# Bucket writes one by one in VectorE's written order, and conditional slots' output writes behind all blocks

## The chip, the cores and the metric

The kernel runs on one core of one Trainium2 chip. The metric is device time in microseconds, from the first to the last instruction of one launch; lower is better. The profile is one further execution of the same program with the hardware profiler on.

## The reference

Two stages in float32. The first is attention with a sliding window over 8 batches, 8 heads, 576 positions and 64 channels. Half of the heads see the last 32 positions, the other half every fourth of the last 128. The second is a mixture of experts without dropped tokens over the 4608 tokens that come out (512 channels each, 8 experts, 1024 hidden channels):

```python
scores = scale * q @ k.T                       # per batch and head
scores = np.where(mask, scores, -1e9)          # plain or dilated window
x = softmax(scores) @ v                        # -> (4608, 512)
logits = x @ w_gate
expert_idx = np.argmax(logits, axis=1)
gate_w = softmax(logits)[arange(N), expert_idx]
for e in range(8):                             # tokens of expert e
    y[tokens_e] = np.maximum(x[tokens_e] @ w1[e], 0) @ w2[e]
out = gate_w[:, None] * y
```

## The kernel before, in words

**Attention and routing.** `attention()` walks through 32 units: 8 batches (called blocks b), two kinds of head, two pairs each. For a unit, TensorE makes scores (L360), ScalarE exponentials (L397), GpSimd multiplies by the reciprocal of the sum (L412), and TensorE turns the result (L422) and multiplies by v (L437). When the four units of a block are done, `route(b)` picks the expert of each of its 576 tokens, in six tiles of 96. It works out the row that each token gets in a table in HBM, `bucket`, which keeps 4608 rows for each expert. The row numbers are made as floats in `dest`, cast to integers in `idx` (L622), and `to_bucket` (L223) then issues six indirect writes on GpSimd, one for each tile. A bucket row has 514 floats: the token's 512 channels, its gate weight and its number.

**Tables.** After some blocks (1 to 7), `tables(s)` decides on VectorE which full slots of 128 rows of one expert can already be computed. The last one, after block 7, lays out all that is left (`pairs` and `mixing` serve two slots that take rows of two experts). It also pads: the rows behind each expert's last token, up to a multiple of 128, are filled from `blank` by eight more indirect writes (index tile `padi`, cast at L687), whose token number is out of range, so that their results are dropped.

**Slots.** `moe()` computes the slots: it turns the 128 rows (`across`, L1108 and L1110), multiplies by w1 (L1172), applies ReLU (L1183 on ScalarE, L1192 on VectorE), multiplies by w2 (L1204), scales by the gate weight into `y` (L1211), casts the token numbers into `to` (L1213), and writes the rows to the output with an indirect write on GpSimd (L1216). That write is put into a list, `late`, and issued inside the next slot. Slots 0 to 35 (`SURE` is 36) always run. Slots 36 to 40 stand in blocks under a condition that is read at run time, `tc.If(live[0] > j)`; in this data one of them runs. The rows of a slot are read by `fetch_x` (L1046), the expert weights by `fetch_w` (L1065), four loads of 1 MB for a slot, with two buffers; rows have three buffers.

**Order.** A planner interleaves three Python generators while the program is written: attention, routing (one step after each piece of attention) and slots. Each piece has a charge; a slot costs 14.98 units. After the attention, each routing step is given 2.0 units of slot work:

```python
while routing:
    clock["owed"] = 2.0
    run_slots()
    run_routing()
```

`fetch_x` and `fetch_w` of a slot are written only when its table is finished (`where[j]`), which for slots 24 to 40 is the end of the routing of block 7. The framework then orders the instructions of each engine by readiness and written position, and sets the semaphores. Reads of the bucket wait for the bucket writes of their own and earlier blocks. `tc.keep_in_program_order(i)` holds an instruction at its written place among those of its engine.

Of the kernel before, what the change touches and what calls it, by code (L numbers as in the profile page):

```python
# [2 lines left out]

# [9 lines left out]
F32 = mybir.dt.float32  # L13
I32 = mybir.dt.int32
# [6 lines left out]
B, H, S, DH = 8, 8, 576, 64  # L21
WIN, DIL = 32, 4
STRIP = S // DIL
N, DM, E, F = B * S, H * DH, 8, 1024
# [32 lines left out]
NSLOT = _most_slots()  # L57
NROWS = E * CAP + 128
NOWHERE = 1.0e6
E1 = E + 1  # L60
SURE = N // 128
# [8 lines left out]
LAG = 2  # L70
# [3 lines left out]
MIX = (2, 5)  # L74
STEP = MIX[1] - MIX[0]
J0 = STAGES[-1][1]
assert J0 + MIX[-1] < SURE


def _constants():  # L80
# [77 lines left out]
def kernel(  # L158
# [10 lines left out]
    nc = tc.nc  # L169
# [51 lines left out]
    def to_bucket(idx, rows, b):  # L221
        wrote_bucket(
            nc.gpsimd.indirect_dma_start(  # L223
                out=bucket,
                out_offset=bass.IndirectOffsetOnAxis(ap=idx, axis=0),
                in_=rows,
                in_offset=None,
                bounds_check=NROWS - 1,
                oob_is_err=False,
            ),  # L230
            b,
        )
# [308 lines left out]
    def route(b):  # L541


        row = rows.pop(b)
        lgs = pool.tile([96, 2 * TT], F32, tag="lgs", name="lgs", bufs=1)
        nc.vector.tensor_copy(lgs, logits.pop(b))
        ps = bank("lg")
        for i in range(2):
            nc.tensor.transpose(
                ps[0:TT, 96 * i : 96 * i + 96], lgs[:, TT * i : TT * i + TT], ident[0:96, 0:96]  # L550
            )

        lg = ps[0:TT, 0:192].rearrange("p (i j e) -> p j i e", i=2, j=3)[:, :, :, 0:E]
        yield
        shape = [TT, NT, E]

        def small(name, *dims, dt=F32):
            return pool.tile([TT, *dims], dt, tag=name, name=name)

        def wide(a):  # L560
            return a.unsqueeze(2).broadcast_to(shape)

        def all_tiles(a):
            return a.unsqueeze(1).broadcast_to(shape)

        rev = all_tiles(const("rev", TT))
        top, best, gate = small("top", NT), small("best", NT), small("gate", NT)
        oh, dl = small("oh", NT, E), small("dl", NT, E)
        nc.vector.tensor_reduce(
            out=top.rearrange("p (j i) -> p j i", i=2), in_=lg, axis=AX, op=OP.max  # L570
        )
        nc.vector.tensor_tensor(
            out=dl.rearrange("p (j i) e -> p j i e", i=2),
            in0=lg,
            in1=top.rearrange("p (j i) -> p j i", i=2).unsqueeze(3).broadcast_to([TT, 3, 2, E]),
            op=OP.subtract,
        )

        nc.vector.scalar_tensor_tensor(
            out=oh, in0=dl, scalar=0.0, in1=rev, op0=OP.is_ge, op1=OP.mult  # L580
        )
        nc.vector.tensor_reduce(out=best, in_=oh, axis=AX, op=OP.max)
        nc.vector.tensor_tensor(out=oh, in0=rev, in1=wide(best), op=OP.is_equal)
        nc.scalar.activation(dl, dl, AF.Exp)

        for i in range(NT):
            n = b * NT + i
            nc.vector.tensor_tensor(  # L590
                out=before[:, n + 1], in0=before[:, n], in1=oh[:, i], op=OP.add
            )
        yield
        ps = bank("rank")
        rk = ps[0:TT, 0 : NT * E]
        nc.tensor.matmul(
            rk,
            lhsT=const("tri", TT),
            rhs=oh.rearrange("p t e -> p (t e)"),
            start=True,  # L600
            stop=False,
        )
        nc.tensor.matmul(
            rk,
            lhsT=const("ones", TT)[:, 0:TT],
            rhs=before[:, b * NT : b * NT + NT].rearrange("p t e -> p (t e)"),
            start=False,
            stop=True,
        )
        nc.vector.tensor_reduce(out=gate, in_=dl, axis=AX, op=OP.add)  # L610
        nc.vector.tensor_scalar(gate, gate, 1e-9, None, op0=OP.add)
        nc.vector.reciprocal(row[:, :, DM], gate)
        pick, dest, idx = small("pick", NT, E), small("dest", NT), small("idx", NT, dt=I32)
        nc.vector.tensor_tensor(
            out=pick,
            in0=rk.rearrange("p (t e) -> p t e", e=E),
            in1=all_tiles(const("ecap", TT)),
            op=OP.add,
        )
        nc.vector.tensor_tensor(out=pick, in0=pick, in1=oh, op=OP.mult)  # L620
        nc.vector.tensor_reduce(out=dest, in_=pick, axis=AX, op=OP.add)
        nc.vector.tensor_copy(idx, dest)  # L622
        for i in range(NT):
            to_bucket(idx[:, i : i + 1], row[:, i], b)
        for s, (b2, _, _) in enumerate(STAGES):
            if b2 == b:
                yield
                yield from tables(s)


    where, live, mix = {}, [], {}
# [1 line left out]
    def tables(s):  # L633
# [41 lines left out]
        if last:  # L675

            pad, far = table("pad", E, p=128), table("far", E, p=128)
            padi = table("padi", E, p=128, dt=I32)
            nc.vector.tensor_scalar(pad, cnt, const("row"), None, op0=OP.add)
            nc.vector.scalar_tensor_tensor(  # L680
                out=far, in0=ns, scalar=128.0, in1=pad, op0=OP.mult, op1=OP.is_le
            )
            nc.vector.scalar_tensor_tensor(
                out=pad, in0=far, scalar=NOWHERE, in1=pad, op0=OP.mult, op1=OP.add
            )
            nc.vector.tensor_tensor(out=pad, in0=pad, in1=const("ecap"), op=OP.add)
            nc.vector.tensor_copy(padi, pad)  # L687
            for e in range(E):
                to_bucket(padi[:, e : e + 1], blank, b)

        av, us = avail[0:1], used[0:1]
        if last:
# [152 lines left out]
        for name, a in (("exi", ex), ("basei", base), ("newi", new)):  # L845
            i = mpool.tile([1, K], I32, tag=f"{name}{s}", name=name, bufs=1)
            nc.vector.tensor_copy(i, a)
            ints.append(i)
        for j in range(j0, j1):
            where[j] = (b, j - j0, *ints)  # L850

# [250 lines left out]
    def moe():  # L1102
# [7 lines left out]
            nc.vector.tensor_copy(xt, ps)  # L1110
            return xt

        late = []
        xt = None
        for j in range(NSLOT):
            if j >= SURE:

                while late:
                    late.pop(0)()
                guards.close()  # L1120
                guards.enter_context(tc.If(live[0] > j))
# [74 lines left out]
            for f in range(8):  # L1196
# [10 lines left out]
                    fetch()  # L1207
                if f < 7:
                    yield 0.88
            y = mpool.tile([128, DM], F32, tag="yo", name="y")  # L1210
            nc.scalar.activation(y, py, AF.Copy, scale=x[:, DM : DM + 1])  # L1211
            to = mpool.tile([128, 1], I32, tag="to", name="to", bufs=3)
            nc.vector.tensor_copy(to, x[:, DM + 1 : ROW])  # L1213

            def scatter(y=y, to=to):
# [8 lines left out]
                tc.declare_no_dep(i, group="out", reason="no token is in two slots")  # L1224
                tc.add_to_no_dep_group("out", i)

            late.append(scatter)
            done[1] = 2 * j + 2
            fetch()
            xt = nxt  # L1230
            yield 0.88
        while late:
            late.pop(0)()
        guards.close()

# [85 lines left out]
```

## Time and profile before

| What | us |
|---|---|
| median of 3 timed runs (lowest to highest) | 813.89 (812.27 to 816.31) |
| the profiled execution, its own time | 856.16 |
| its span, first to last instruction | 854.4 |
| TensorE busy (share of the span) | 780.1 (91%) |
| VectorE / ScalarE / GpSimd busy | 285.2 / 226.2 / 143.6 |
| bucket writes of token rows, 48 at 0.93 | 44.6 |
| pad writes, 8 at 0.98 | 7.9 |
| output writes, 37 at 1.00 | 36.9 |

PE is TensorE, PEld its weight loads, DVE VectorE, ACT ScalarE, POOL GpSimd, and SP the engine that issues most transfers. A group line of the profile gives source line, engine, operation, output and inputs, count, busy time and mean, and then the idle time just before these instructions and what ended it. "issue" stands for idle time in which the engine waited for nothing that the profile shows. A line of a stretch gives its bounds, its length, the busy time of each engine, the share of full clock that was granted to TensorE, the share of time in which the 16 DMA engines were busy, and the rate in GB/s.

### The profile page before, as it was taken

The page shows a single profiled execution, that of the slowest core. Times are in us where ns is not written, and L with a number is a line of the kernel's source. Part 1 is how long each engine was busy: PE and PEld are TensorE (multiplying, and loading weights), DVE is VectorE, ACT ScalarE, POOL GpSimd, SP SyncE. Part 2 cuts the span into 40 slices and gives each one's busy share as a digit, 9 for nine tenths or more (in the row PEclk, how much of TensorE's full clock was granted, in tenths as well). Part 3 has the DMA queues.
Part 4 walks back from the last instruction along what each step waited for, and adds up shares of the span by engine and source line. Part 5 has one row for each costly group of instructions (what it writes and reads, how often), then busy time and mean ns, then how long its engine had stood idle before and what let it go on. Part 6 is the DMA issues. An engine that isn't in the chain of part 4 may idle for free.

```text
span 854.4 us, 17984 instructions
## 1 busy us (share of the span) xinstructions
PE 780.1 (91%) x6838; PEld 565.5 (66%) x6838; DVE 285.2 (33%) x954; ACT 226.2 (26%) x853; POOL 143.6 (17%) x137
## 2 busy tenths in 40 slices
PE   4898787999999999998999989969999999999991
PEld 3676566677677767776777767746868374577770
DVE  2675665545532433344332432225111100111010
ACT  1775652523332323331222321200001001010100
POOL 0224423113111221112111220060000000000000
PEclk9898989899999999998999999979999999999996
DMA  9877589899998969876247447769993393894993
GB/s 194 184 153 180 148 260 320 199 310 244 289 267 288 291 199 299 271 241 209 68 142 247 138 162 230 263 219 310 326 326 123 123 321 108 290 298 133 308 338 131
DMA packets 165516, 195.40 MB, mean 229 GB/s; under 512 B 73200, under 2 KB 87280, under 8 KB 165426
## 3 DMA queue, kind: packets, MB, share of 16 engines
q1 hardware_dynamic: 153156, 169.00, 66.3%
q0 software_dynamic: 6672, 19.71, 6.5%
q10 hardware_dynamic: 5598, 5.48, 2.4%
q8 instruction: 57, 0.93, 0.4%
q14 instruction: 33, 0.27, 0.1%
HBM read 216.14 MB, written 21.54 MB: 278 GB/s over the span
## 4 chain that ended last, share of the span: by engine, by line
PE 47%; issue 38%; ACT 4%; POOL 4%; DMA 2%; DVE 2%; POOLq 0%; ACTq 0%
PE ph L1172 14%; PE py L1204 13%; PE scores L360 4%; PE xo L437 3%; PE weights L422 3%; ACT e L397 3%; POOL out_dram L1216 2%; PE xrow L523 2%; PE turned L311 2%; DMA k<-in_k_dram 2%; PE logits L533 2%; PE turned L319 1%; POOL bucket L223 1%; PE xt L1108 1%; DMA bucket<-rows,idx 1%
## 5 line engine op out<-in xcount | busy, mean ns | idle before, releaser
L1172 PE MATMUL ph<-xt,w 128*128 128x128 f32 x2240 | 277.8, 279 | 4.8 <-issue 4.4
L1172 PEld LDWEIGHTS ph<-xt,w 128*128 128x128 f32 x2240 | 264.1, 193 | 22.6 <-issue 19.3
L1204 PE MATMUL py<-w,h 128*128 128x512 f32 x560 | 268.4, 614 | 7.9 <-issue 6.7
L1204 PEld LDWEIGHTS py<-w,h 128*128 128x128 f32 x560 | 101.2, 194 | 107.6 <-issue 101.1
L1216 POOL DMA_INDIRECT out_dram<-y,to x37 | 36.9, 997 | 405.3 <-ACT y L1211 371.8
L1211 ACT ACTIVATE y<-py,x 128x512 f32<-128x512 f32 x37 | 25.4, 685 | 252.6 <-PE py L1204 214.8
L412 POOL TENSOR_TENSOR e<-e,rec 128x864 f32<-128x864 f32 x32 | 52.2, 1630 | 197.3 <-DVE rec L411 109.3
L1110 DVE COPY xt<-xt 128x512 f32<-128x512 f32 x38 | 26.2, 691 | 160.0 <-PE xt L1108 155.2
L397 ACT ACTIVATE e<-e,lo 128x96 f32<-128x96 f32 x144 | 52.0, 363 | 80.8 <-DVE lo L389 80.5
L424 DVE COPY eT<-weights 96x384 f32<-96x384 f32 x96 | 48.2, 547 | 66.7 <-PE weights L422 66.5
L397 ACT ACTIVATE e<-scores,lo 128x96 f32<-128x96 f32 (+1 forms) x160 | 52.1, 346 | 26.7 <-DVE lo L376 26.2
L223 POOL DMA_INDIRECT bucket<-rows,idx x48 | 44.6, 930 | 54.5 <-DVE idx L622 32.6
L437 PEld LDWEIGHTS xo<-eT,v 96*64 96x64 f32 x1216 | 40.1, 138 | 20.5 <-issue 11.0
L437 PE MATMUL xo<-eT,v 96*64 96x64 f32 (+1 forms) x1216 | 46.9, 225 | 2.6 <-issue 2.6
L360 PE MATMUL scores<-kT,qT 64*64 64x96 f32 x1152 | 41.1, 267 | 6.9 <-issue 6.9
L422 PE MATMUL weights<-ident,e 128*96 128x128 f32 x288 | 40.0, 283 | 7.5 <-issue 4.0
L1183 ACT ACTIVATE h<-ph 128x512 f32<-128x512 f32 x35 | 20.9, 597 | 93.9 <-PE ph L1172 84.2
L360 PEld LDWEIGHTS scores<-kT,qT 64*64 64x64 f32 x1152 | 35.4, 147 | 14.5 <-issue 11.7
L422 PEld LDWEIGHTS weights<-ident,e 128*96 128x96 f32 x288 | 32.7, 131 | 14.4 <-issue 10.1
L1192 DVE TENSOR_SCALAR h<-ph 128x512 f32<-128x512 f32 x35 | 24.2, 691 | 42.7 <-PE ph L1172 42.5
L382 DVE TENSOR_TENSOR e<-scores,masks 128x384 f32<-128x384 f32 x64 | 23.0, 400 | 32.4 <-PE scores L360 23.5
L397 ACT ACTIVATION_READ_ACCUMULATOR e<-scores,lo 128x1 f32 (+1 forms) x160 | 33.6, 210 | 0.0
(206 smaller groups left out, 586.1 us busy)
## 6 DMA issues: line engine op xcount, KB each, us to landing
w<-in_moe_w_dram SPq DMA_DIRECT2D x164, 1024.0 KB
x<-bucket SPq DMA_DIRECT2D x26, 257.0 KB
v<-in_v_dram SPq DMA_DIRECT2D x32, 192.0 KB
q<-in_q_dram SPq DMA_DIRECT2D x32, 144.0 KB
q<-in_q_dram SPq DMA_DIRECT2D x8, 576.0 KB
v<-in_v_dram SPq DMA_DIRECT2D x48, 96.0 KB
k<-in_k_dram SPq DMA_DIRECT2D x28, 144.0 KB
k<-in_k_dram SPq DMA_DIRECT2D x7, 576.0 KB
```

The source lines that it names most:

```text
L223: nc.gpsimd.indirect_dma_start(out=bucket, out_offset=bass.IndirectOffsetOnAxis(ap=idx, axis=0), in_=rows, in_offset=None, bounds_check=NR ...
L360: nc.tensor.matmul(sc[r][64 * c : 64 * c + 64, 96 * (i % 5) : 96 * (i % 5) + 96], lhsT=qT[rows, 64 * j : 64 * j + 64], rhs=kT[rows, first_ ...
L397: nc.scalar.activation(out=e[p0:p1, i], in_=s[:, 96 * (i - i0) : 96 * (i - i0) + 96], func=AF.Exp, bias=lo[p0:p1, i : i + 1], scale=-1.0, ...
L412: nc.gpsimd.tensor_tensor(out=e, in0=e, in1=rec.unsqueeze(2).broadcast_to([128, 9, 96]), op=OP.mult)
L422: nc.tensor.transpose(tp[0:96, 128 * i : 128 * i + 128], e[:, a + i], ident)
L424: nc.vector.tensor_copy(eT, tp[0:96, 0:384])
L437: nc.tensor.matmul(xo[DH * h : DH * h + DH, at0 : at0 + nq], lhsT=vt[:, 2 * hl + r, j, :] if ty == 0 else vt[:, hl, j, DH * r : DH * r + D ...
L1110: nc.vector.tensor_copy(xt, ps)
L1172: nc.tensor.matmul(ph[:, fi], lhsT=w1[:, c, 128 * f : 128 * f + 128], rhs=xt[:, c], start=c == 0, stop=c == 3,)
L1204: nc.tensor.matmul(py, lhsT=h[:, f], rhs=w2[:, f], start=f == 0, stop=f == 7)
L1211: nc.scalar.activation(y, py, AF.Copy, scale=x[:, DM : DM + 1])
L1216: i = nc.gpsimd.indirect_dma_start(out=out, out_offset=bass.IndirectOffsetOnAxis(ap=to, axis=0), in_=y, in_offset=None, bounds_check=N - 1 ...
```

## The change

Three edits. (1) In `route`, the one cast of six columns becomes six casts of one column, each held at its written place on VectorE and followed by its bucket write. A routing step ends after each write, and the pieces of `tables` are taken one by one between the writes and not after them. (2) The eight pad writes of the last table move from its first piece to its end, again one cast, one write and one routing step at a time, before `where[j]` is set. (3) The output writes of slots 36 to 40 are issued after the last conditional block is closed, all five of them whatever the condition was. To that end each of these slots has a `y` and a `to` of its own, set ahead of the first conditional block to zeros and to a row number out of range; they lie in buffers that the attention no longer uses. An imported name and an assertion that bounds the number of conditional slots complete it.

```diff
--- before.py
+++ after.py
@@ -1,5 +1,5 @@
 from contextlib import ExitStack
-from itertools import combinations_with_replacement
+from itertools import chain, combinations_with_replacement
 
 import ml_dtypes
 import numpy as np
@@ -74,7 +74,7 @@
 MIX = (2, 5)
 STEP = MIX[1] - MIX[0]
 J0 = STAGES[-1][1]
-assert J0 + MIX[-1] < SURE
+assert J0 + MIX[-1] < SURE and NSLOT - SURE <= 6
 
 
 def _constants():
@@ -619,13 +619,16 @@
         )
         nc.vector.tensor_tensor(out=pick, in0=pick, in1=oh, op=OP.mult)
         nc.vector.tensor_reduce(out=dest, in_=pick, axis=AX, op=OP.add)
-        nc.vector.tensor_copy(idx, dest)
+
+
+        pieces = chain.from_iterable(tables(s) for s in range(len(STAGES)) if STAGES[s][0] == b)
         for i in range(NT):
+            tc.keep_in_program_order(
+                nc.vector.tensor_copy(idx[:, i : i + 1], dest[:, i : i + 1])
+            )
             to_bucket(idx[:, i : i + 1], row[:, i], b)
-        for s, (b2, _, _) in enumerate(STAGES):
-            if b2 == b:
-                yield
-                yield from tables(s)
+            yield next(pieces, None)
+        yield from pieces
 
 
     where, live, mix = {}, [], {}
@@ -684,9 +687,6 @@
                 out=pad, in0=far, scalar=NOWHERE, in1=pad, op0=OP.mult, op1=OP.add
             )
             nc.vector.tensor_tensor(out=pad, in0=pad, in1=const("ecap"), op=OP.add)
-            nc.vector.tensor_copy(padi, pad)
-            for e in range(E):
-                to_bucket(padi[:, e : e + 1], blank, b)
 
         av, us = avail[0:1], used[0:1]
         if last:
@@ -846,6 +846,12 @@
             i = mpool.tile([1, K], I32, tag=f"{name}{s}", name=name, bufs=1)
             nc.vector.tensor_copy(i, a)
             ints.append(i)
+        for e in range(E) if last else ():
+            tc.keep_in_program_order(
+                nc.vector.tensor_copy(padi[:, e : e + 1], pad[:, e : e + 1])
+            )
+            to_bucket(padi[:, e : e + 1], blank, b)
+            yield
         for j in range(j0, j1):
             where[j] = (b, j - j0, *ints)
 
@@ -1110,9 +1116,20 @@
             nc.vector.tensor_copy(xt, ps)
             return xt
 
-        late = []
+        late, outs, spare = [], [], {}
         xt = None
         for j in range(NSLOT):
+            if j == SURE:
+
+
+                for i in range(SURE, NSLOT):
+                    a = pool.tile([128, S], F32, tag="xT", name="spare", bufs=3) if i < SURE + 3 \
+                        else pool.tile([128, 9, 96], F32, tag="e", name="spare", bufs=LAG + 1)
+                    if i >= SURE + 3:
+                        a = a.rearrange("p i k -> p (i k)")
+                    spare[i] = a[:, 0:DM], mpool.tile([128, 1], I32, name=f"to_{i}", bufs=1)
+                    nc.vector.memset(spare[i][0], 0.0)
+                    nc.vector.memset(spare[i][1], int(NOWHERE))
             if j >= SURE:
 
                 while late:
@@ -1207,9 +1224,12 @@
                     fetch()
                 if f < 7:
                     yield 0.88
-            y = mpool.tile([128, DM], F32, tag="yo", name="y")
+            if j >= SURE:
+                y, to = spare[j]
+            else:
+                y = mpool.tile([128, DM], F32, tag="yo", name="y")
+                to = mpool.tile([128, 1], I32, tag="to", name="to", bufs=3)
             nc.scalar.activation(y, py, AF.Copy, scale=x[:, DM : DM + 1])
-            to = mpool.tile([128, 1], I32, tag="to", name="to", bufs=3)
             nc.vector.tensor_copy(to, x[:, DM + 1 : ROW])
 
             def scatter(y=y, to=to):
@@ -1224,14 +1244,14 @@
                 tc.declare_no_dep(i, group="out", reason="no token is in two slots")
                 tc.add_to_no_dep_group("out", i)
 
-            late.append(scatter)
+            (late if j < SURE else outs).append(scatter)
             done[1] = 2 * j + 2
             fetch()
             xt = nxt
             yield 0.88
-        while late:
-            late.pop(0)()
         guards.close()
+        for scatter in outs:
+            scatter()
```

## The prediction

> **What bounds the kernel now.** I read the page's busy shares and slices first, then busy time by stretch of time, then the timeline where a stretch falls short, then the sequencers' own instructions at the end.
>
> The page says that TensorE carries the time:
>
> ```profile
> span 854.4 us, 17984 instructions
> PE 780.1 (91%) x6838; PEld 565.5 (66%) x6838; DVE 285.2 (33%) x954; ACT 226.2 (26%) x853; POOL 143.6 (17%) x137
> ...
> PEclk9898989899999999998999999979999999999996
> ...
> L223 POOL DMA_INDIRECT bucket<-rows,idx x48 | 44.6, 930 | 54.5 <-DVE idx L622 32.6
> ```
>
> PE is busy 91% of 854.4 us. VectorE at 33% and GpSimd at 17% have room. The clock digits drop below 9 in places, and those places are the subject. The 48 bucket writes come in eight groups of six (one group per attention block b), the last followed by eight pad writes. Busy time by stretch, cut around four of the eight groups and around an undisturbed stretch (length, then PE, PEld, DVE, ACT, POOL busy, clock, DMA share, GB/s):
>
> ```profile
> 63.00:78.00 15.00, 11.64 (x128) 8.62 (x126) 7.19 (x22) 5.73 (x27) 7.60 (x8) 0.78 0.76 189
> 140.00:158.00 18.00, 13.30 (x122) 9.07 (x122) 7.55 (x38) 5.17 (x25) 7.48 (x8) 0.72 0.95 211
> 488.00:504.00 16.00, 11.75 (x97) 9.28 (x96) 8.48 (x37) 2.44 (x8) 6.55 (x7) 0.89 0.38 110
> 556.00:580.00 24.00, 16.35 (x70) 9.79 (x70) 8.53 (x65) 0.60 (x1) 13.92 (x15) 0.72 0.65 207
> 600.00:650.00 50.00, 50.00 (x301) 37.55 (x301) 5.96 (x11) 4.45 (x7) 2.93 (x3) 1.00 0.93 309
> ```
>
> Without bucket writes PE is full at clock 1.00. With them it isn't. Over all eight stretches the idle time (length minus PE busy) is 3.4+4.0+4.7+2.5+1.6+2.7+4.3+7.7 = 30.9 us. Half-speed time adds busy x (1 - clock): 2.6+2.5+3.7+0+0+2.9+1.3+4.6 = 17.6 us. Together 48.5 us. What happens inside is in the timelines of PE and VectorE in the last group:
>
> ```profile
> 571.25 1.01 PE L1204 MATMUL py<-w,h 128*128 128x512 f32 x1 [1.61 <-issue]
> 572.68 1.01 PE L1204 MATMUL py<-w,h 128*128 128x512 f32 x1 [0.42 <-issue]
> 574.09 1.21 PE L1204 MATMUL py<-w,h 128*128 128x512 f32 x1 [0.40 <-issue]
> ...
> 571.27 0.18 DVE L917 TENSOR_TENSOR scratch<-scratch 1x32 f32<-1x32 f32 x1 [1.15 <-DVE scratch L725]
> 571.99 0.25 DVE L731 TENSOR_REDUCE scratch<-scratch 1x34 f32<-1x102 f32 x1 [0.54 <-issue]
> 573.39 0.19 DVE L925 TENSOR_REDUCE scratch<-scratch 1x8 f32<-1x32 f32 x1 [1.15 <-DVE scratch L731]
> 574.09 0.17 DVE L734 SCALAR_TENSOR_TENSOR scratch<-scratch 1x17 f32<-1x17 f32 x1 [0.51 <-DVE scratch L925]
> ```
>
> No tile is late ("issue"). Two unrelated engines start single instructions on one beat of about 0.7 us (571.25 and 571.27, 574.09 and 574.09). [...]
>
> **Is that stall in the timed runs?** This decides the forecast. The profiled execution took 856.16 us (span 854.4); the timed median is 813.89, 42.3 us less. Elsewhere there is little to give back: a 512-column matmul of L1204 starts every 0.43 us in the undisturbed slots, and idle time outside the groups is the first load (15 us), the tail (18 us) and some 11 us more. So of the 48.5 us about 42 must be missing from the timed runs; 48.5 - 42.3 = 6.2 us at most remain. I take the beat for the cost of recording, not of the kernel.
>
> [...] GpSimd's waits on bucket landings after a group reach 8.3 us, 22.6 in four, mean 5.7.
>
> **The change, part by part.**
>
> *Six index casts for one, one write after each, spread over six routing steps.* The one L622 cast (172 ns) becomes six of about 0.15 us (the one-column cast of L1213 is 146 ns): 40 more casts, 6 us of VectorE in all, beside a third-busy engine: 0. The same 48 writes of 0.93 us stay on GpSimd. Their spreading frees GpSimd for the softmax product L412, but that work was not held: at 63.9 to 71.1 the group ends, and the next L412 waits 3.7 us more for its reciprocal. PE's wait on L412 is 3.5 us in the whole span. Value 0; bounds -2 and +3 (each pinned cast keeps its written place on VectorE, and with it holds the later evictions of that engine; GpSimd's next product queues behind the write that waits for it). If spreading halves the remaining 6.2 us of stall: -3.0; bounds -6 and 0.
>
> *Table pieces run between the writes, pads last.* One routing call fewer in blocks 1 to 6: 0. In block 7 the written steps after the rank are 25 instead of 18. Each lets the planner run about 2.7 units of a 14.98-unit slot, 0.18 slot. By its charges block 7 closes at slot 22.2 before and about 23.6 after; the last pad is written at about slot 23.4. Slot 24's rows are the first that need this table and wait for all bucket writes of block 7. Today's issue is early:
>
> ```profile
> 613.00 0.35 SPq L1046 DMA_DIRECT2D x<-bucket  x1
> ...
> 629.62 0.60 PE L1108 MATMUL xt<-ident,x 128*128 128x128 f32 x4
> ...
> 640.50 3.73 PE L1172 MATMUL ph<-xt,w 128*128 128x128 f32 x32
> ```
>
> x of slot 24 leaves SP at 613.0, is turned inside slot 23 at 629.6, and slot 24 starts at 640.5. After: the last pad is cast at 626.0 + 0.44 x 14.5 = 632.4, generated by 633.7[...], and the read takes about 2.3 us (one issued at 583.95 is turned at 586.27): ready at 638 to 644. The turning moves to the head of slot 24, so PE waits for the copy L1110 (0.69 us and about 0.3 of handover): +1.0. [...] no further wait. Bounds 0 and +9 (below). SP runs the weight loads of slot 24 in this stretch; I take them to pass ahead, as they don't read the bucket. GpSimd has nothing else then.
>
> *Conditional slots' writes always issued behind all blocks.* Five conditional slots (36 to 40), one of them live. The skipped blocks now settle their missing writes one by one on GpSimd:
>
> ```profile
> L1120 POOLq INC_SWDGE_SEM  x3: 2000/2012/2022, 837.2 to 841.6; - x3
> L1234 POOLq INC_SWDGE_SEM  x1: 2006/2006/2006, 843.8 to 843.8; - x1
> ...
> L1319 POOLq DRAIN  x3: 51/107/7670, 845.9 to 854.1; - x3
> ```
>
> Four of 2.0 us fill 837.2 to 845.8; a drain of 7.7 us follows, and the end. After: four more L1216 writes at 0.98 + 0.30 = 1.28 us behind slot 36's at 837.07, so GpSimd is free at 843.2 instead of 845.8: -2.6. The drain isn't explained by the trace. If it works off what the four increments leave, it goes too (bound -10); if it must retire five writes instead of one, it grows by four times 1.2 (bound +2). Five zero fills of 128x512 (L190: 0.49 us) and five small ones are 3 us of VectorE, which is 12% busy there: 0.
>
> Sum: -3.0 + 0 + 1.0 - 2.6 = -4.6 us, 813.9 to **809.3** timed. The profiled execution should fall far more, by 20 to 40 us.
>
> **Rivals.**
> - *The stall is real without the profile.* For: it is in the trace. Against: the 42 us and the unchanged matmul pace. It would give 813.9 minus 10 to 40: about 790.
> - *Slower: the last pads hold slot 24.* Place: SP before slot 24. If the landing takes 8.3 us, x is ready at 644.3 instead of 640.5: +3.8; if slot 24's weight loads stand behind it on SP, the first (1 MB at 309 GB/s, 3.4 us[...]) arrives 5 to 7 us late[...]: with the 1.0, +9, and nothing saved in the stall: about 820. It decides once x leaves SP later than about 638. Pinned casts that delay evictions in the attention stage push the same way.
> - *Nothing to be seen*: the increments run as long elsewhere in the drain, the stall wasn't there: 813 to 815.
>
> **How the numbers follow.** 0.5% is 4.1 us, about what a measurement of this kernel can tell. Main case 0.60 (809.3, own range 804 to 815: 0.55 faster, 0.40 same, 0.05 slower); stall real 0.10 (faster); nothing 0.08 (same); slower 0.22 (0.82 slower, 0.15 same, 0.03 faster). Faster 0.33+0.10+0.01 = 0.44; same 0.24+0.08+0.03 = 0.35; slower 0.21. The range takes in the slow case to 822 and part of the real-stall case: 794 to 822.
>
> **What would show it.** Right: bucket writes several us apart on GpSimd, shorter "issue" gaps in the eight stretches, no INC_SWDGE_SEM, five L1216 writes at the end, GpSimd at its drain some 2.6 us sooner, the turning of slot 24's rows at that slot's head. Wrong: a timed gain of over 10 us (the stall was real), or idle PE before slot 24 with x or w as its releaser.

## The result and the profile after

| | median, us (lowest to highest) | ratio to before, 95% interval |
|---|---|---|
| before | 814.42 (812.27 to 816.31) | |
| changed | 821.69 (821.00 to 826.27) | 1.0102 [1.0057, 1.0147] |

The changed kernel is 7.3 us slower, by four executions of each kernel; the forecast was 4.6 us faster. One plain fact is needed to read all that follows: the kernel before is not equally fast on every chip. Unaltered, it ran 814.8 and 815.8 us on two chips of the experiments and 814.4 in this comparison, but 855.5 to 856.5 on three others, in timed executions. These are called 815-chips and 856-chips below; "chip" takes in the host around it, since no run tells the two apart. Which chips the first comparison met isn't on record. By its time, the 856.16 us that the prediction started from is that of an 856-chip, and the 813.89 beside it that of an 815-chip. After's profile (its execution took 821.52 us) is that of an 815-chip, so the two pages must not be subtracted. From the page of the kernel after, the lines that answer to those shown of before:

```profile
span 819.8 us, 18060 instructions
PE 763.7 (93%) x6838; PEld 558.7 (68%) x6838; DVE 284.8 (35%) x1011; ACT 225.8 (28%) x853; POOL 147.7 (18%) x141
...
PEclk9999999999899999999999999999989999999996
...
L1236 POOL DMA_INDIRECT out_dram<-y,to x36 | 36.0, 1000 | 378.8 <-ACT y L1232 354.8
L223 POOL DMA_INDIRECT bucket<-rows,idx x48 | 44.8, 933 | 76.3 <-DVE upto L701 26.3
L1233 DVE CAST to<-x 128x1 int32<-128x1 f32 x37 | 5.4, 146 | 100.2 <-DMA x<-bucket 96.4
```

The clock row has two digits below 9 ahead of its end, where before's had six. This isn't the change's work: the unaltered kernel's row on an 815-chip (before_again, below) has two as well. The last line matters later: before the token-number cast `to`, VectorE is idle for 96.4 us in all, waiting for slot rows. Most of that costs nothing, as before_again has much of it too:

```profile
L1213 DVE CAST to<-x 128x1 int32<-128x1 f32 x37 | 5.5, 149 | 95.9 <-DMA x<-bucket 80.7
```

One of these waits costs. Stretches of the kernel after, around the first, fifth and last group (start:end, length, busy time of PE, PEld, DVE, ACT and POOL with the number of instructions, clock, DMA share, GB/s):

```profile
62.00:77.00 15.00, 15.00 (x264) 11.93 (x254) 12.25 (x40) 12.57 (x58) 9.25 (x9) 1.00 0.92 238
283.00:299.00 16.00, 16.00 (x147) 12.87 (x145) 10.07 (x43) 5.79 (x23) 7.33 (x7) 1.00 0.69 188
528.00:552.00 24.00, 24.00 (x153) 18.41 (x151) 17.57 (x135) 1.88 (x3) 8.52 (x10) 1.00 1.01 358
```

PE is full in all three. The loss lies elsewhere, around the start of slot 24. Timelines of the kernel after (start, length, instruction, and in brackets the idle time before it and its releaser), first SyncE's transfers:

```profile
585.46 0.35 SPq L1052 DMA_DIRECT2D x<-bucket  x1
586.22 2.64 SPq L1071 DMA_DIRECT2D w<-in_moe_w_dram  x4
589.11 2.68 SPq L1052 DMA_DIRECT2D x<-bucket  x1
```

Then VectorE, in the same kernel:

```profile
602.51 0.15 DVE L1233 CAST to<-x 128x1 int32<-128x1 f32 x1 [9.75 <-DMA x<-bucket]
602.58 0.68 DVE L1116 COPY xt<-xt 128x512 f32<-128x512 f32 x1
```

And TensorE:

```profile
598.68 0.60 PE L1114 MATMUL xt<-ident,x 128*128 128x128 f32 x4
603.32 6.52 PE L1189 MATMUL ph<-xt,w 128*128 128x128 f32 x32 [4.04 <-DVE xt L1116]
```

Read them as one chain. The rows of slot 24 leave SyncE at 585.46, when slot 23 has just begun (before: 613.00, 13 us ahead of its slot 23). The four weight loads of slot 24 stand behind them, and behind these 4 MB the rows of slot 25. Slot 24's rows are there in time (VectorE casts their token numbers at 588.31) and are turned at 598.68. But their copy L1116 stands on VectorE behind the `to` cast of slot 25, which waits 9.75 us for those last rows. TensorE idles 4.04 us and restarts at half clock (0.50 granted from 602.25 to 608.75): 32 matmuls of `ph` take 6.52 us instead of 3.73.

The tail has changed as described. The timeline of GpSimd in the kernel after:

```profile
804.80 0.97 POOL L1236 DMA_INDIRECT out_dram<-spare,to  x1 [13.48 <-ACTq L1137]
806.08 0.98 POOL L1236 DMA_INDIRECT out_dram<-spare,to  x1 [0.31 <-issue]
...
809.92 0.97 POOL L1236 DMA_INDIRECT out_dram<-spare,to  x1 [0.30 <-issue]
```

And the drains of its sequencer, by the view of their source line (count, shortest, median and longest in ns, first and last start):

```profile
L1339 POOLq DRAIN  x3: 51/113/11178, 807.7 to 819.5; - x3
```

Five writes 1.28 us apart, no increments, and the drain ends 8.0 us after the last of them (818.9 after 810.9).

### The profile page after: what moved, and what is told of

Read it like the earlier page. It is cut to its first block, busy times and chain, and to the rows that moved or that the text cites. A ratio compares the mean times of both kernels' runs of the same rounds, so it can differ in the third digit from the quotient of the medians.

```text
span 819.8 us, 18060 instructions
## 1 busy us (share of the span) xinstructions
PE 763.7 (93%) x6838; PEld 558.7 (68%) x6838; DVE 284.8 (35%) x1011; ACT 225.8 (28%) x853; POOL 147.7 (18%) x141
## 4 chain that ended last, share of the span: by engine, by line
PE 46%; issue 36%; DMA 5%; ACT 4%; POOL 4%; DVE 3%; SPq 1%; POOLq 0%; ACTq 0%
PE ph L1189 15%; PE py L1221 13%; PE xo L437 3%; PE scores L360 3%; PE weights L422 3%; ACT e L397 3%; POOL out_dram L1236 2%; DMA x<-bucket 2%; PE xrow L523 2%; PE turned L319 2%; DMA k<-in_k_dram 2%; PE turned L311 1%; PE logits L533 1%; PE xt L1114 1%; DMA out_dram<-y,to 1%
## 5 line engine op out<-in xcount | busy, mean ns | idle before, releaser
L1189 PEld LDWEIGHTS ph<-xt,w 128*128 128x128 f32 x2240 | 266.2, 195 | 22.2 <-issue 15.1
L1221 PE MATMUL py<-w,h 128*128 128x512 f32 x560 | 259.2, 599 | 0.0
L1221 PEld LDWEIGHTS py<-w,h 128*128 128x128 f32 x560 | 99.1, 190 | 93.8 <-issue 89.0
L1116 DVE COPY xt<-xt 128x512 f32<-128x512 f32 x38 | 26.1, 687 | 138.4 <-PE xt L1114 138.2
L1200 ACT ACTIVATE h<-ph 128x512 f32<-128x512 f32 x35 | 20.9, 596 | 92.4 <-PE ph L1189 84.0
L1233 DVE CAST to<-x 128x1 int32<-128x1 f32 x37 | 5.4, 146 | 100.2 <-DMA x<-bucket 96.4
L360 PEld LDWEIGHTS scores<-kT,qT 64*64 64x64 f32 x1152 | 32.4, 141 | 8.7 <-issue 4.5
L360 PE MATMUL scores<-kT,qT 64*64 64x96 f32 x1152 | 36.7, 257 | 0.0
```

What stands on the lines that cost most here:

```text
L360: nc.tensor.matmul(sc[r][64 * c : 64 * c + 64, 96 * (i % 5) : 96 * (i % 5) + 96], lhsT=qT[rows, 64 * j : 64 * j + 64], rhs=kT[rows, first_ ...
L1189: nc.tensor.matmul(ph[:, fi], lhsT=w1[:, c, 128 * f : 128 * f + 128], rhs=xt[:, c], start=c == 0, stop=c == 3,)
L1221: nc.tensor.matmul(py, lhsT=h[:, f], rhs=w2[:, f], start=f == 0, stop=f == 7)
```

## The experiments

Times are medians; "gap n" is the time from the end of the `y` eviction of slot n-1 to that of slot n (an undisturbed full slot: 14.4 to 14.5 us).

### Is the stall in the timed executions?

**only_outs, only_spread, pads_first, pads_late_at_once.** The edits taken apart. The first has edit 3 alone, the second edit 1 alone (pads as before). The other two have edits 1 and 3 and write the eight pads in one burst, early or at the table's end:

```diff
 pads_first: after, without the eight steps, and behind the line that adds "ecap" to pad
+            nc.vector.tensor_copy(padi, pad)
+            for e in range(E):
+                to_bucket(padi[:, e : e + 1], blank, b)
 pads_late_at_once: after, with those lines at the table's end instead of the eight steps
```

> The kernel before with the third edit alone: the output writes of the conditional slots stand behind all blocks. Theory (the late pads cost 7 us at slot 24, the third edit saves its 2.4 us of tail as the trace of the changed kernel shows): 2 to 3 us faster than before, about 811.8, and GpSimd reaches its last drain with four index writes in place of the four increments. Rival (the third edit also costs something before the tail, such as zero fills in VectorE's way at slot 36): equal to before or slower, with idle PE in slots 35 and 36.

> The kernel before with the first edit alone: six casts held in place, one bucket write each, table pieces between them; pads as before. Theory (the stall of the profile is a cost of recording): the profiled execution loses most of its 40 us over the timed runs, while the timed median stays within 4 us of before, 810 to 818. Rival 1 (the held casts hold back evictions on VectorE and so PE): timed 4 to 8 us slower, with idle PE in the attention stage, above all the 6 us at 200 us of the changed kernel's trace. Rival 2 (spreading removes a real stall): timed 6 us faster or more.

> The changed kernel with the pad writes back in the first piece of the last table, as one cast and eight writes (first and third edit stay). Theory (late pads hold slot 24's rows and, behind them on SP, its weights): slot 24 follows slot 23 after 14.5 us in place of 21.8, and the median falls by 7 to 9 us below the changed kernel, to 812 to 815. Rival (the loss lies in the held casts and the table pieces between the writes): stays above 818.

> The changed kernel with the pad writes at the end of the last table, but as one cast and eight writes at once without a routing step after each, so that the table closes about 1.2 slots sooner in the written order. Theory (what hurts is how late the last pad stands, by the eight steps and the held casts, not that the pads stand behind the table): as fast as with the pads first, 812 to 816. Rival (being behind the table is enough, since the table's end and eight writes of 1.3 us each come too late): 3 us or more slower than with the pads first.

Measured, on one chip where before ran 856.53: only_outs 853.78, ratio 0.9963 [0.9947, 0.9980]; only_spread 837.65, 0.9804 [0.9773, 0.9834]; pads_first 838.36, 0.9816 [0.9794, 0.9838]; pads_late_at_once 834.62, 0.9742 [0.9714, 0.9769]. Timed executions of before took as long here as the profiled one of the prediction, and spreading the writes takes 19 us off. On such a chip the stall is a real cost. Edit 3 gives its 2.8 us. In all four traces gap 24 is 14.4 us: without edit 2 as it stands in the changed kernel, slot 24 isn't late. In pads_late_at_once the one cast isn't held, and its pads run from 552.28 to 567.26, among and right behind the bucket writes: written late, they aren't late in time.

Much of what is left of the stall sits in the pads' burst: gap 19 is 27.2 us in pads_first (28.6 before). The timeline of GpSimd in that burst of pads_first:

```profile
547.74 0.97 POOL L223 DMA_INDIRECT bucket<-blank,padi  x1 [0.30 <-issue]
549.02 0.97 POOL L223 DMA_INDIRECT bucket<-blank,padi  x1 [0.30 <-issue]
550.30 0.97 POOL L223 DMA_INDIRECT bucket<-blank,padi  x1 [0.30 <-issue]
```

And that of TensorE, same kernel:

```profile
545.63 1.88 PE L1218 MATMUL py<-w,h 128*128 128x512 f32 x4
556.76 3.78 PE L1218 MATMUL py<-w,h 128*128 128x512 f32 x4 [9.25 <-DVE idx L627]
```

And of VectorE:

```profile
556.02 0.69 DVE L1206 TENSOR_SCALAR h<-ph 128x512 f32<-128x512 f32 x1 [8.47 <-remote]
```

GpSimd writes on every 1.28 us while TensorE stands for 9.25 us. What TensorE waits for is `h`, the input of these matmuls: VectorE's ReLU L1206 ends at 556.71, just before they start. VectorE itself has stood for 8.47 us, with "remote" as releaser, which names no instruction. only_spread, pads_first_2, pads_first_3 and bare_steps show the same wait of VectorE, 8.4 to 9.7 us long.

**after_again, after_3.** The changed kernel unaltered, twice on 856-chips.

> The changed kernel unaltered, beside before. In the first comparison before ran 814 us and the changed kernel 822; on another chip before ran 856 us. Theory: the freezes behind groups of bucket writes are in the timed runs of some chips and absent on others, and the late slot 24 (+7 us) is always there. Where before runs 856 us this kernel then runs 828 to 840 us (ratio 0.97 to 0.98), where before runs 814 us it runs 819 to 824 (ratio 1.005 to 1.013). Rival: the loss of the first comparison depends on the chip alone, and then the ratio here says nothing on slot 24: its gap in the trace from the end of slot 23 to that of slot 24 would be below 16 us.

> The changed kernel once more, for its ratio beside the two parts of it in this call. Where before runs about 815 us: 820 to 825 us; where it runs 856: 828 to 836. Gap from the end of slot 23 to that of slot 24 20 us or more on either.

Measured: 831.66 us, ratio 0.9695 [0.9658, 0.9732], and 829.32, ratio 0.9723 [0.9683, 0.9763]. The same change that loses 1% on an 815-chip saves 3% here. Gap 24 is 20.8 and 20.9 us (21.8 in the first comparison): the late slot is there on either kind of chip.

**before_again.** Before, unaltered, with a trace; it met an 815-chip (815.84 timed).

> The kernel before, unaltered, for its trace on this chip. Where it runs 856 us its trace shows idle and half-clock time in all eight groups of bucket writes, some 48 us in sum, as in the profile shown first. Where it runs 814 us the theory (the freezes are absent on such a chip, timed or profiled) says that this sum is below 10 us and the first slot ends some 16 us earlier; the rival (the profile makes them) says that the trace shows them on any chip and that the profiled execution is some 40 us over the timed ones.

Measured: 818.64 us for the profiled execution, 2.8 above the timed median, not 40. From its page:

```profile
span 816.8 us, 17984 instructions
...
PEclk9999989999999989999999999999999999999996
```

And the stretches around its first, fifth and last group:

```profile
62.00:77.00 15.00, 15.00 (x265) 11.86 (x265) 11.70 (x32) 13.22 (x62) 9.23 (x9) 1.00 0.94 238
278.00:296.00 18.00, 15.50 (x120) 12.24 (x118) 9.10 (x41) 5.30 (x22) 8.45 (x9) 0.85 0.81 230
528.00:552.00 24.00, 23.20 (x156) 18.68 (x156) 17.04 (x125) 2.33 (x4) 15.46 (x16) 1.00 1.02 351
```

Same program, same bursts, profiler on, and PE is full or nearly so. Over all eight groups 6.8 us are idle and 2.3 lost to half clock, 9.1 against 48.5; 2.5 us of these are a wait for slot rows in the fifth stretch. The first slot ends 19.8 us earlier (148.6 against 168.4). On an 856-chip the two agree as well (only_outs: 855.65 profiled, 853.78 timed). So the recording doesn't make the stall; the kind of chip decides. One of the 856-chips was met twice and was one both times.

**wide_rows.** Before, with bucket rows of 528 floats instead of 514 (2112 bytes; the added columns repeat the token number). It asks whether the length of the rows makes the stall, the "freezes" of the expectation.

```diff
 wide_rows, its first part:
-ROW = DM + 2
+ROW = 528
```

> The kernel before, with bucket rows of 528 instead of 514 elements ([...] the extra columns hold copies of the token number, and the output is unchanged). Theory: [...] they go, and the time is 812 to 820 us where before runs 856. Rival: they come from many indirect writes in a row, whatever their length: the time stays within 5 us of before. Where before runs 814 us neither shows anything.

Measured on an 856-chip: 854.97, ratio 0.9997 [0.9980, 1.0014]. The stall is there with either length of row: in the stretches 63 to 78, 488 to 504 and 556 to 580, TensorE is idle for 16.7 us of 55, against 15.3 in before.

### What makes slot 24 late?

**bare_steps.** Pads early in a burst, eight empty routing steps at the table's end.

```diff
 pads_first, and at the table's end
+        for e in range(E) if last else ():
+            yield
```

> Pads written first in the table, as before, and eight empty routing steps at the table's end. Theory: slot 24 is late because the pad writes stand late and its row read waits for them; with the pads early the empty steps cost nothing, and the gap from the end of slot 23 to that of slot 24 is 14.5 to 16 us. Rival: the eight steps alone put the slots' reads late (the table's integers are there only after them): gap 20 us or more.

Measured on an 856-chip: gap 24 is 15.9 us. The rows are turned only at the slot's head, as the timeline of TensorE in bare_steps shows:

```profile
624.73 0.60 PE L1113 MATMUL xt<-ident,x 128*128 128x128 f32 x4
626.11 3.84 PE L1188 MATMUL ph<-xt,w 128*128 128x128 f32 x32 [0.78 <-DVE xt L1115]
```

So the steps alone make slot 24 1.5 us longer, and slot 23, which no longer does this turning, 0.4 us shorter (14.0). For both together that is 29.9 us instead of 28.9, 1.0 more. The other 5 us of slot 24 come from the writes. The time is 836.97 (0.9742 [0.9702, 0.9782]), with the burst's loss back in gap 19 (27.0).

**pads_late_not_held.** The changed kernel without the hold on the eight casts.

```diff
-            tc.keep_in_program_order(
-                nc.vector.tensor_copy(padi[:, e : e + 1], pad[:, e : e + 1])
-            )
+            nc.vector.tensor_copy(padi[:, e : e + 1], pad[:, e : e + 1])
```

> The changed kernel, with the eight pad casts not held to their written place on VectorE. Theory: the casts then move up on VectorE ahead of the h evictions, the eight pad writes run well before slot 23, the read of slot 24 leaves SP some 10 us before slot 23 starts, and the gap from the end of slot 23 to that of slot 24 is 14.5 to 16 us: 5 to 8 us less than the changed kernel of this call. Rival: the written steps place the writes, held or not: the gap stays at 20 us or more, and the time within 2 us of the changed kernel.

Measured, same chip: gap 24 is 15.9, so the holding behind VectorE's written order is what makes the pads late. But the time, expected 5 to 8 us under the changed kernel, is 836.20 (0.9731 [0.9697, 0.9765]), 4.5 us over it, with intervals that overlap. The freed casts move up, the writes join the bucket writes to one train, and gaps 19 and 20 grow from 16.1 and 15.1 to 21.6 and 17.3. On this chip, what holding costs at slot 24 it saves in the burst.

**pads_between.** Each pad write behind one of the later table pieces, still held.

```diff
 pads_between: after, without the eight steps; pads is a list of the eight columns
-        yield from pieces
+        for piece in pieces:
+            if pads:
+                i, a = pads.pop(0)
+                tc.keep_in_program_order(nc.vector.tensor_copy(i, a))
+                to_bucket(i, blank, b)
+            yield piece
```

> The changed kernel, with each pad write behind one of the later pieces of the last routing table instead of in eight steps of its own behind it: still held to its written place, still one at a time. Theory: neither a burst of eight nor a late slot 24: gap from the end of slot 18 to that of slot 19 15 to 17 us, from slot 23 to slot 24 14.4 to 16 us. Against the changed kernel 5 to 7 us less: 824 to 828 us where before runs 856, 811 to 816 where before runs 814. Rival: the held casts stand behind the evictions wherever they are written, and the last pads come as late as in the changed kernel: gap before slot 24 20 us or more, time within 2 us of the changed kernel.

> The kernel with each pad write behind one of the later table pieces, again. Where before runs 856 us, theory (no burst, no late slot 24): 823 to 828 us, 4 to 8 less than the changed kernel there (829 and 832); rival: within 2 us of it. Where before runs 815: 818 to 822 as before, and the trace shows what its lower, profiled run of before left out: reads of early slots' rows late by 5 us or more.

Measured: 820.39 on an 815-chip (1.0057 [1.0033, 1.0082]) and 834.03 on an 856-chip (0.9755 [0.9716, 0.9795]); both above the theory's values. Gap 24 is 14.4 in both, as expected. The pads only moved the loss: on the 856-chip gap 20 is 21.6 us. The timeline of GpSimd in pads_between_2:

```profile
548.32 0.98 POOL L223 DMA_INDIRECT bucket<-blank,padi  x1 [1.28 <-DVE avail L973]
549.61 0.98 POOL L223 DMA_INDIRECT bucket<-blank,padi  x1 [0.30 <-DVE scratch L761]
550.90 0.98 POOL L223 DMA_INDIRECT bucket<-blank,padi  x1 [0.30 <-issue]
```

And that of TensorE, same kernel:

```profile
556.25 0.27 PE L1190 MATMUL ph<-xt,w 128*128 128x128 f32 x1 [0.34 <-issue]
556.97 0.36 PE L1190 MATMUL ph<-xt,w 128*128 128x128 f32 x1 [0.45 <-issue]
557.67 0.37 PE L1190 MATMUL ph<-xt,w 128*128 128x128 f32 x1 [0.34 <-issue]
```

Apart in the program isn't apart in time: the pieces ran close together and the writes were 1.28 us apart. Some 7 us into that train the beat of 0.7 us is back.

**rows_on_gpsimd.** The changed kernel; the rows of slots 24 and 25 are read by GpSimd's queue.

```diff
-            queue = nc.sync
+            queue = nc.gpsimd if j in (J0, J0 + 1) else nc.sync
```

> The changed kernel, with the row reads of slots 24 and 25 alone issued by GpSimd instead of SyncE; the pad writes stay late. Theory: the larger part of slot 24's delay is that its weight loads stand behind its row read on SyncE, and the rows of slot 25 behind those weights. They then leave SyncE without waiting for the pads, and the gap from the end of slot 23 to that of slot 24 falls from 21 to 15 or 16.5 us (rows turned at the slot's head, 1 to 2 us). Rival: the rows of slot 24 are themselves late (pads landed too late), wherever they are issued: the gap stays at 19 us or more.

Measured on an 815-chip: 823.66 (1.0085 [1.0059, 1.0111]). Gap 24 falls to 15.9, but gap 23 rises to 21.3: the loss moved one slot ahead, so the run settles nothing. The timeline of VectorE in slot 23 of this kernel:

```profile
595.67 0.15 DVE L1233 CAST to<-x 128x1 int32<-128x1 f32 x1 [16.65 <-DMA x<-bucket]
598.76 0.15 DVE L1233 CAST to<-x 128x1 int32<-128x1 f32 x1 [2.93 <-DMA x<-bucket]
598.87 0.69 DVE L1209 TENSOR_SCALAR h<-ph 128x512 f32<-128x512 f32 x1
```

And that of TensorE:

```profile
599.62 6.57 PE L1221 MATMUL py<-w,h 128*128 128x512 f32 x8 [4.11 <-DVE h L1209]
```

Two `to` casts now stand ahead of slot 23's own ReLU, and the rows came later still (read at 590.08 instead of 585.46).

**w1_before_rows.** The changed kernel; on SyncE two of slot 24's weight loads stand ahead of its rows.

```diff
+        elif j == J0:
+            wanted += w[0:2] + [x]
+            w = w[2:]
         else:
             wanted.append(x)
         wanted += w
```

> The changed kernel with one move in SyncE's order: the two loads of slot 24's first weights stand ahead of the read of its rows, instead of behind it; pads stay late. Theory: slot 24 is late because its weights, and behind these the rows of slot 25, whose token cast stands ahead of slot 24's row copy on VectorE, leave SyncE only after the read that waits for the last pads. Then the gap from the end of slot 23 to that of slot 24 falls from 21 to between 14.5 and 16.5 us, VectorE's wait for the rows of slot 25 falls from some 10 us to below 4, and the time is 4 to 6 us below the changed kernel: 823 to 827 us where before runs 856, 816 to 819 where it runs 815. Rival: the rows of slot 24 are themselves too late: gap 19 us or more, time within 2 us of the changed kernel.

Measured on an 815-chip (before 814.81): 817.98, ratio 1.0042 [1.0021, 1.0063]. Gap 24 is 15.9 us. The timeline of SyncE in this kernel:

```profile
588.92 0.35 SPq L1052 DMA_DIRECT2D x<-bucket  x1
589.67 1.13 SPq L1071 DMA_DIRECT2D w<-in_moe_w_dram  x2
591.05 0.35 SPq L1052 DMA_DIRECT2D x<-bucket  x1
```

Of VectorE:

```profile
599.41 0.15 DVE L1236 CAST to<-x 128x1 int32<-128x1 f32 x1 [3.08 <-DMA x<-bucket]
602.88 0.69 DVE L1119 COPY xt<-xt 128x512 f32<-128x512 f32 x1 [3.32 <-PE xt L1117]
```

And of TensorE:

```profile
603.63 3.84 PE L1192 MATMUL ph<-xt,w 128*128 128x128 f32 x32 [0.78 <-DVE xt L1119]
```

The pads are as late as ever, and the rows of slot 24 leave 0.7 us into slot 23 (588.92, slot 23 starting at 588.23), against 0.8 in the changed kernel. Still the copy L1119 now waits for TensorE and not behind a cast, and `ph` runs at full clock. So the weights and the next rows behind the row read made 5.9 of the 21.8 us of slot 24; with the rows as late as ever, what is left is the turning, as in bare_steps. The median came out at the middle of the expected range, but its interval just touches that of the changed kernel (1.0057 to 1.0147): the gap is shown by the trace, the size of the timed gain only roughly. And it is still 3.2 us above before, with slot 24 mended.

### Which edit costs the rest on an 815-chip?

**only_outs_2, only_outs_3, pads_first_2, pads_first_3.** The same kernels as above, to split the loss on an 815-chip. All four met 856-chips.

> The third edit alone (outputs of the conditional slots behind all blocks), as in an earlier run where before ran 856 us and this edit took 2.8 us off. Theory: it does the same on any chip: 812 to 813.5 us where before runs 815. Rival: its gain lay under the freezes, and where they are absent nothing is seen (within 0.7 us of before).

> The third edit alone. Where before runs 815 us: 812 to 813.5 if its gain is that of the tail on any chip, within 0.7 us of before if it lay under the freezes. Where before runs 856: 853 to 854.5, as in two earlier calls.

> The first and third edits together, pads in one burst early as before. The kernel with the pads between the pieces kept the first and third edits, had no late slot 24, and was still 4.6 us over before where before runs 816. Theory: spreading the bucket writes itself costs where the freezes are absent (the pinned casts and the routing steps that they shift put rows of early slots late): 816 to 820 us where before runs 815, against 812 to 813.5 with the third edit alone. Rival: the spread writes cost nothing, and that loss came from pads between the pieces: then 811 to 814 here. Where before runs 856 us: 836 to 840.

> The first and third edits together. Where before runs 815 us, theory (spreading the writes itself costs some 5 us there): 816 to 821; rival (spreading costs nothing there, the loss came with pads between the pieces): 811 to 814. Where before runs 856: 833 to 839, as in two earlier calls.

Measured: edit 3 alone 853.71 (0.9979 [0.9968, 0.9990]) and 853.80 (0.9970 [0.9953, 0.9988]); edits 1 and 3 together 834.30 (0.9774 [0.9730, 0.9817]) and 835.33 (0.9766 [0.9725, 0.9806]). They repeat the first results and leave the question for 815-chips open.

## Why the prediction was wrong, point by point

The best pair of traces is before_again and after, both from 815-chips. From the ends of the `y` evictions (each figure rounded by itself):

| from, to | before_again, us | after, us | difference |
|---|---|---|---|
| start to slot 3 | 224.0 | 225.1 | +1.1 |
| slots 4 to 18 | 304.5 | 302.1 | -2.4 |
| slots 19 to 23 | 75.4 | 72.4 | -3.0 |
| slot 24 | 14.4 | 21.8 | +7.4 |
| slots 25 to 36 | 181.0 | 183.1 | +2.1 |
| tail behind slot 36 | 17.6 | 15.3 | -2.3 |
| span | 816.8 | 819.8 | +3.0 |

**Pads last, +1.0: this is the step that failed.** Slots 23 and 24 together take 35.8 us in after and 28.9 in before: 7.0 instead of 1.0. The turning at the slot's head did cost the 1.0: bare_steps and w1_before_rows take 29.9 us for the two slots. The prediction's dates were near as well: it had the last pad generated 7.7 us into slot 23, and it was 2.1 us ahead of it (582.6, slot 23 starting at 584.7); x left SyncE 2.8 us after that, where GpSimd's waits on landings of token rows took 3.92 to 8.31 us in before. The early end of "638 to 644" was the author's estimate. What failed is "no further wait" with its reason, "I take them to pass ahead, as they don't read the bucket". The weights are written behind the row read, and on SyncE they leave behind it (585.46 and 586.22). w1_before_rows shows that this choice is worth 5.9 us. This step makes 6.0 of the 11.9 us between the forecast of -4.6 and the +7.3 measured; the rest isn't placed (see "What stays open").

**The rival "last pads hold slot 24" came true**, with 821.7 against its 820, and the measured time lies inside 794 to 822 only because the range took this rival in. Its place was right, its chain was not, and that its sum came so near is partly luck: its +9, in part the author's estimate, was 7.0, and time that nobody has placed made up the rest. It had slot 24's own weights arrive late. In the trace the late part is slot 25's rows, 4 MB behind, acting through a cast on VectorE that slot 24 doesn't need. The restart at half clock cost 2.8 us (6.52 instead of 3.73). Its deciding point was off too: it wanted x to leave SyncE 12 us into slot 23 (638 of a slot that starts at 626.0). It decided at 0.8 us.

**"I take the beat for the cost of recording": wrong.** The comparison of 856.16 with 813.89 was, by its times, one of two kinds of chip. Timed executions of 856 us on three chips and a profiled one of 818.64 on an 815-chip show it. That recording makes the beat was the author's estimate; no run shows it. Nor do all engines keep to the beat: GpSimd writes on every 1.28 us while TensorE stands for 9.25 us (pads_first). The "unchanged matmul pace" is seen: 16 matmuls of 512 columns take 7.03 us in before and in after, whose profiled execution (821.52) lies among its other three (821.00 to 826.27). It holds with the stall real as well. The rival "the stall is real without the profile" (about 790) is true of 856-chips, where the change saves 24 to 26 us, not of the comparison that was forecast.

**Spreading, -3.0:** in the pair of traces slots 4 to 23 are 5.4 us shorter, of which 2.5 are a wait for slot rows that comes and goes and 0.4 the turning that left slot 23. No timed run on an 815-chip shows a gain. On an 856-chip it gives 19. It spreads less than it says: the first six writes stay 1.2 to 1.4 us apart (63.03 to 69.37 in after), and on an 856-chip after_again still loses time there, as this stretch shows:

```profile
64.00:78.00 14.00, 10.53 (x117) 7.71 (x115) 6.64 (x22) 5.75 (x27) 7.46 (x8) 0.77 0.80 197
```

**Conditional outputs, -2.6: right in the traces.** From the end of slot 36's `y`, GpSimd is done after 6.4 us instead of 9.0. The span gets 2.3. On 856-chips edit 3 alone gave 2.8, 1.8 and 2.0; alone on an 815-chip it wasn't measured. The drain, which the prediction couldn't explain, is 7.7 us behind the increments and 8.0 behind the last write: neither bound (-10, +2) was touched.

**What stays open.** Slot 24 isn't the whole loss on an 815-chip. w1_before_rows (gap 24 15.9) and pads_between (14.4) are still 3.2 and 4.6 us above before, both clear of noise, where -4.6 was forecast. Which edit costs this isn't known: the kernels that take the edits apart met only 856-chips. The traces differ by 3.0 us, the medians by 7.3. before_again's profiled execution is 4.2 us above the median of before in the first comparison, which covers the difference in size; what makes it so wasn't shown. A candidate is seen in TensorE's waits between 195 and 212 us. In before_again:

```profile
PE xt L1108 <- DMA x<-bucket: 3.8, 1, 3.8
```

And in the kernel after:

```profile
PE xt L1114 <- DMA x<-bucket: 6.2, 1, 6.2
```

The read of slot 3's rows leaves SyncE at 189.95 and 192.68 behind weights and q and k, and takes 15.4 and 14.2 us. In w1_before_rows and rows_on_gpsimd the wait is 5.0 and 5.2. In pads_between's fastest execution (811.85, the one profiled, 8.5 below its median) this wait is absent. How often each kernel meets it wasn't measured. The 1.5 us that w1_before_rows and the changed kernel lose at the mixed slot 29 come and go as well: with edit 3 alone gap 29 is 18.3, 19.9 and 18.3. What makes a chip an 815- or an 856-chip wasn't found.

No kernel tried is shown to beat before on an 815-chip. On 856-chips the changed kernel is the lowest measured, 829.3 and 831.7, with intervals that overlap those of the next ones.

## What to carry to other kernels

When the profiled execution and the timed ones differ by several per cent, first run the unchanged kernel again elsewhere: the difference may be the chip's and not the profiler's. When a load is made to wait, list what is written behind it on the same queue, whether it needs the data or not, and then what waits for that; here a cast for the next slot waited 9.75 us and stopped the copy of this one. Steps apart in the program need not be apart in time: read the distances of the writes from the timeline (1.28 us in pads_between_2).

## What the runs showed of the hardware

On 856-chips, when a train of indirect writes 1.2 to 1.3 us apart has run for some 3 to 7 us (first idle time of TensorE at 67.0 of a train from 63.88 in before, at 547.5 of one from 540.17 in pads_first), other engines start single instructions or short runs on a beat of about 0.7 us (556.25, 556.97 and 557.67 in pads_between_2), or stand (VectorE 8.47 us in pads_first, and TensorE behind it). On 815-chips the same trains cost 2 to 3 us at most (gap 20 of pads_between 16.9, of pads_between_2 on an 856-chip 21.6; gaps 19 and 20 of before_again 16.4 and 15.3). The changed kernel writes its pads one and three at a time, and the gaps in which they lie, 20 and 22, are 14.4 to 15.1 us on either kind. Rows of 514 and of 528 floats give the same time (855.82 and 854.97, ratio 0.9997). The mechanism wasn't found.

A row read of 0.26 MB behind four weight loads of 1 MB takes 13.4 us (589.11, cast at 602.51), one behind two of them 8.4 us (591.05, cast at 599.41 in w1_before_rows), and one ahead of them 2.9 us (588.92, cast at 591.79, same kernel): all three are of one size, and in these traces the place in the queue makes the difference.
